# FNet mixing and squared relu on one core: column 128 of seven sequences transformed in one pass instead of one pass each

## The chip, the cores and the metric

The kernel runs on one core of a Trainium2 chip. Times are device microseconds (us) of one execution. Ratios are the mean time of one kernel's fast runs over the mean of the fast runs of the kernel before in the same rounds, so they are not quite the ratios of the medians quoted beside them. PE is TensorE's matmuls, PEld its weight loads, DVE the vector engine, ACT the scalar engine, SP the engine that issues most DMAs here.

## The reference, cut to what matters

```python
X = np.fft.fft(np.fft.fft(x, axis=1), axis=2).real   # x: (8, 3008, 256) float32
h = X.reshape(24064, 256) @ w_in                     # w_in: (256, 2048)
g = np.maximum(h, 0) ** 2
out = g @ w_out                                      # w_out: (2048, 256)
```

The weights arrive as float64.

## The kernel before

The transform over the 256 columns is folded into w_in once. The transform over the 3008 rows is done for each sequence b as matmuls with cosine and sine tables. Symmetry folds x to 753 rows and to columns 0..128: P takes columns 0..127 (cosine), Q takes 1..127 (sine), and column 128 has a transform of its own, E. E enters h as a product of one row, which DVE adds, and so it must lie alike on all 128 partitions. The kernel gets that by copying column 128 of the folded x to 128 stationary columns (wE), so that the matmul itself spreads it:

```python
def fold(b, t):                      # tile t of sequence b; DVE, with two small copies on ACT
    ...
    nc.scalar.copy(wE[r], wP[r, :, H:H + 1].to_broadcast([rows, 2, P]))
    folded[b, t] = (wP, wQ, wE)
...
for kp in range(2):                  # parity of k
    for which in range(3):           # P, Q, E: each an even_n and an odd_n item of three matmuls
        ops += group(kp, which, {})
```

The main loop runs 96 units for each sequence: 6 blocks of columns k by 16 chunks of d_ff. A unit makes h (front), and three units later the output matmuls of an earlier unit follow (back). In between, the folds and the transform of the *next* sequence are strewn in as "side work", evenly over 88 of the 96 units:

```python
for i, (k0, n, fc) in enumerate(units):
    if b == 0 and k0 == 0 and fc % 2 == 0:
        load_wout(fc)                # DVE rounds a piece of w_out from float64
    flight.append((b, k0, n, fc, front(b, k0, n, fc)))
    if len(flight) > LAG:            # LAG = 3
        back(*flight.pop(0))
    upto = min(len(side), len(side) * (i + 1) // (len(units) - 8))
    for f in side[done:upto]:
        f()
    done = upto
```

Of the kernel before, what the change touches and what calls it, by code (L numbers as in the profile page):

```python
# [7 lines left out]
F32 = mybir.dt.float32  # L8
U32 = mybir.dt.uint32
AF = mybir.ActivationFunctionType  # L10
ALU = mybir.AluOpType
PSUM = bass.MemoryType.PSUM
P = 128

# With P(k, m) = sum_n x[n, m] cos(2 pi k n / S) and Q(k, m) the same with sin,
#   Re FFT2(x)[k, d] = sum_m P(k, m) cos(2 pi m d / D) - Q(k, m) sin(2 pi m d / D).
# * The transform over d is linear and sits before w_in, so it is applied to w_in, once:
#   h[k] = P(k) @ (cosD @ w_in) - Q(k) @ (sinD @ w_in).
# * cos and sin are even and odd in m, so columns m and D - m of x fold: P keeps m = 0..128 and
#   Q keeps m = 1..127. Column 128 of P, called E, has a one-row product with w_in, added apart.  # L20
# * P is even and Q is odd in k, so k = 0..S/2 gives all rows: h[S - k] = P-part - Q-part.
# * In n, the rows n, S - n, S/2 - n and S/2 + n share a table row for k of one parity: x folds to
#   n = 0..S/4. With even n in A and odd n in B, P(S/2 - k) = A - B where P(k) = A + B
#   (Q: B - A), so that tables are needed for k = 0..S/4 alone.
# The weights come as float64, of which the chip has no arithmetic: their bits are sent, and rounded
# to float32 on the chip.


def row_tiles(S):
    """Even n, then odd n, of 0..S/4, in tiles of at most 128 rows: (first row, rows) of the folded order."""  # L30
    q = S // 4
    tiles, at = [], 0
    for count in (q // 2 + 1, q // 2):
        assert 2 * P < count <= 3 * P
        for r in range(0, count, P):
            tiles.append((at + r, min(P, count - r)))
        at += count
    return tiles
# [3 lines left out]
def kernel(  # L42
# [12 lines left out]
    nc = tc.nc  # L55
    B, NROW, _, D = x.shape
    S = out.shape[0] // B
    M = S // 2
# [16 lines left out]
    hp = ctx.enter_context(tc.tile_pool(name="hp", bufs=3))  # L75
    gp = ctx.enter_context(tc.tile_pool(name="gp", bufs=5))
    op = ctx.enter_context(tc.tile_pool(name="op", bufs=4))
    psh = ctx.enter_context(tc.tile_pool(name="psh", bufs=3, space=PSUM))
    psd = ctx.enter_context(tc.tile_pool(name="psd", bufs=2, space=PSUM))
    pso = ctx.enter_context(tc.tile_pool(name="pso", bufs=3, space=PSUM))  # L80
# [1 line left out]
    tt = nc.vector.tensor_tensor  # L82
    act = nc.scalar.activation

# [1 line left out]
    xt = {}  # L86

    def load_x(b, t):
# [19 lines left out]
        for tab, src in ((cosT, cos_s), (sinT, sin_s)):  # L108
            nc.gpsimd.dma_start(out=tab[:, kp], in_=src[:, kp])

# [1 line left out]
    def rounded(dst, src):  # L112
        """The float32 next to each float64 of src, [128, 2, 256] of them as 64-bit words in DRAM."""
        if src.dtype == F32:
            nc.sync.dma_start(out=dst, in_=src)
            return
        raw = op.tile([P, 2, CH, 2], U32, name="raw", tag="raw", bufs=2)
        nc.sync.dma_start(out=raw.rearrange("p a b w -> p a (b w)"), in_=src.bitcast(U32))
        low, high = raw[:, :, :, 0], raw[:, :, :, 1]

        def temp(tag):
            t = fp.tile([P, 2, CH], F32, name=tag, tag=tag)
            return t, t.bitcast(U32)

        # Sign, exponent and the first 20 bits of the fraction, to float32's places.
        top, topb = temp("fs")
        nc.vector.tensor_scalar(out=topb, in0=high, scalar1=3, scalar2=0x3FFFFFF8,  # L127
                                op0=ALU.logical_shift_left, op1=ALU.bitwise_and)
        nc.vector.scalar_tensor_tensor(out=topb, in0=high, scalar=0xC0000000, in1=topb,  # L129
                                       op0=ALU.bitwise_and, op1=ALU.bitwise_or)  # L130
        # The other 32 bits as a number, in units of 2^-52 of the signed power of two.
        rest, restb = temp("fd")
        nc.vector.tensor_scalar(out=restb, in0=topb, scalar1=0xFF800000, scalar2=None, op0=ALU.bitwise_and)  # L133
        nc.vector.scalar_tensor_tensor(out=rest, in0=low, scalar=2.0 ** -52, in1=rest, op0=ALU.mult, op1=ALU.mult)  # L134
        tt(out=top, in0=top, in1=rest, op=ALU.add)  # L135
        # Exponents out of float32's range: to zero and to infinity.
        over, _ = temp("fs")
        _, expb = temp("fd")
        nc.vector.tensor_scalar(out=expb, in0=high, scalar1=20, scalar2=0x7FF,  # L139
                                op0=ALU.logical_shift_right, op1=ALU.bitwise_and)  # L140
        nc.vector.tensor_scalar(out=over, in0=expb, scalar1=1150.5, scalar2=2.0 ** 127,  # L141
                                op0=ALU.is_gt, op1=ALU.mult)
        nc.vector.scalar_tensor_tensor(out=top, in0=expb, scalar=896.5, in1=top, op0=ALU.is_gt, op1=ALU.mult)  # L143
        nc.vector.scalar_tensor_tensor(out=dst, in0=over, scalar=1.0, in1=top, op0=ALU.max, op1=ALU.mult)  # L144

# [1 line left out]
    WC = 512  # L147
    for c in range(F // WC):
        cs = slice(c * WC, (c + 1) * WC)
# [17 lines left out]
        rounded(wout[:, fc:fc + 2],  # L167
                moe_w_out[fc * P:(fc + 2) * P].rearrange("(c p) e -> p c e", p=P))

# [1 line left out]
    folded = {}  # L171
    PQE = {}

    def fold(b, t):
        """Rows n, S - n, M - n, M + n and columns m, D - m of x, to the terms of even and of odd k."""
        rows = TILES[t][1]
        r = slice(0, rows)
        v = xt[b, t]
        s = fp.tile([P, 2, D], F32, name="fs", tag="fs")
        d = fp.tile([P, 2, D], F32, name="fd", tag="fd")  # L180
        tt(out=s[r], in0=v[r, 0::2], in1=v[r, 1::2], op=ALU.add)
        tt(out=d[r], in0=v[r, 0::2], in1=v[r, 1::2], op=ALU.subtract)  # L182
        if b + 1 < B:
            load_x(b + 1, t)
        sc = fp.tile([P, 2, H + 1], F32, name="sc", tag="sc")
        dc = fp.tile([P, 2, H - 1], F32, name="dc", tag="dc")
        nc.scalar.copy(sc[r, :, 0:H + 1:H], s[r, :, 0:H + 1:H])
        tt(out=sc[r, :, 1:H], in0=s[r, :, 1:H], in1=s[r, :, D - 1:H:-1], op=ALU.add)
        tt(out=dc[r], in0=d[r, :, 1:H], in1=d[r, :, D - 1:H:-1], op=ALU.subtract)
        wP = wp.tile([P, 2, H + 1], F32, name="wP", tag="wP")  # L190
        wQ = wp.tile([P, 2, H - 1], F32, name="wQ", tag="wQ")
        wE = wp.tile([P, 2, P], F32, name="wE", tag="wE")
        for kp in range(2):
            tt(out=wP[r, kp], in0=sc[r, 0], in1=sc[r, 1], op=ALU.subtract if kp else ALU.add)  # L194
            tt(out=wQ[r, kp], in0=dc[r, 0], in1=dc[r, 1], op=ALU.add if kp else ALU.subtract)
        nc.scalar.copy(wE[r], wP[r, :, H:H + 1].to_broadcast([rows, 2, P]))  # L196
        folded[b, t] = (wP, wQ, wE)

    def dft_ops(b):
        """P, Q and, on all partitions alike, E, for k = 0..M."""  # L200
        ops = []

        def start():
# [2 lines left out]

        def group(kp, which, st):
            nk = NK[kp]
            n = P - 1 if which == 1 else P
            tab = sinT if which == 1 else cosT  # L210

            def product(half):
                ps = psd.tile([P, 512], F32, name="pd", tag="d")[0:n, 0:nk]
                for i in range(3):
                    t = 3 * half + i
                    rows = TILES[t][1]
                    nc.tensor.matmul(ps, folded[b, t][which][0:rows, kp, 0:n], tab[0:rows, kp, t, 0:nk],  # L217
                                     start=i == 0, stop=i == 2)
                return ps

# [4 lines left out]

            def odd_n():
                ps = product(1)
                a, dst = st["a"], PQE[b][which]
                nh = S // 8
                tt(out=dst[:, kp:kp + 2 * nk - 1:2], in0=a, in1=ps, op=ALU.add)  # L230
                hi = dst[:, M - kp - 2 * (nh - 1):M - kp + 1:2][:, ::-1]
# [5 lines left out]
            return [even_n, odd_n]  # L237

        for kp in range(2):
            for which in range(3):  # L240
                ops += group(kp, which, {})
        return [start] + ops

# [1 line left out]
    def front(b, k0, n, fc):  # L245
        pt, qt, et = PQE[b]
        fs = slice(fc * P, (fc + 1) * P)
# [19 lines left out]
    def back(b, k0, n, fc, g):  # L267
# [11 lines left out]
        for s, (g0, cnt, row) in enumerate(sides):  # L279
# [5 lines left out]
            for j, o in enumerate(range(0, cnt, P)):  # L285
                m = min(P, cnt - o)
                nc.scalar.copy(os_[0:m, j], po[s][0:m, j])
                nc.sync.dma_start(out=out[row + o:row + o + m], in_=os_[0:m, j])

    def ahead(b):  # L290
        return [lambda t=t: fold(b, t) for t in range(NT)] + dft_ops(b)

    for f in ahead(0):
        f()
# [3 lines left out]
    for b in range(B):  # L298
        side = ahead(b + 1) if b + 1 < B else []
        done = 0  # L300
        for i, (k0, n, fc) in enumerate(units):
            if b == 0 and k0 == 0 and fc % 2 == 0:
                load_wout(fc)
            flight.append((b, k0, n, fc, front(b, k0, n, fc)))
            if len(flight) > LAG:
                back(*flight.pop(0))
# [11 lines left out]


def _tables(S, D):  # L320
    """The cosines and sines of the transforms, which depend on the shapes alone."""
    import numpy as _np

    q = S // 4
    n = _np.concatenate([_np.arange(0, q + 1, 2), _np.arange(1, q + 1, 2)])
    weight = _np.where((n == 0) | (n == q), 0.5, 1.0)[:, None]  # their four rows of x are two rows twice
    tabs = _np.zeros((2, P, 2, 6, q // 2 + 1), _np.float32)
    for kp in range(2):
        k = _np.arange(kp, q + 1, 2)
# [46 lines left out]
```

## Time and profile before

| | before |
|---|---|
| time, median | 2299.17 us |
| PE busy | 2213.2 us, 96% |
| DVE busy | 1182.4 us, 51% |
| ACT busy | 1049.4 us, 46% |
| E matmuls, 8 sequences | 192 records, about 7.6 us a sequence |

The prediction shows the lines that carry the reading. Kernel before:

```profile
PEld po L275 <- ACT os L282: 6.1, 33, 0.2
PEld po L275 <- ACT os L287: 2.0, 7, 0.3
```

These are the block ends. The second bank of a new block is free only when ACT has copied the old one. Each such wait was 0.2 us at most (0.3 us on the second line, the short last block of a sequence, which is the same after the change), so it looked harmless.

### The profile page before, as it was taken

How to read it: one execution, taken by the hardware profiler on the slowest of the kernel's cores; microseconds unless marked ns; L12 is line 12 of the kernel's file. 1: busy time of each engine (PE TensorE's matmuls, PEld its weight loads, DVE VectorE, ACT ScalarE, POOL GpSimd, SP SyncE). 2: the span in 40 equal slices, each digit the busy share in tenths (PEclk: the TensorE clock that was granted, in tenths of full speed). 3: DMA queues.
4: the chain of work that ended last, by engine and by line, in shares of the span. 5: the costliest groups of instructions: out<-in, count | busy, mean ns of one | idle time of the engine just before them, and what ended most of it. 6: DMA issues, size and time to landing. Idle time of an engine off the chain costs nothing.

```text
span 2298.1 us, 26257 instructions
## 1 busy us (share of the span) xinstructions
PE 2213.2 (96%) x9888; PEld 1865.0 (81%) x9888; DVE 1182.4 (51%) x2932; ACT 1049.4 (46%) x1809; POOL 28.1 (1%) x56
## 2 busy tenths in 40 slices
PE   3679999999999999999999999999999999999998
PEld 1357888888888888888888888888888888888887
DVE  5597444654446544474445644465444644444443
ACT  0124444554445444454445544455444544445554
POOL 0000000000000000000000000000000000000000
PEclk7789999999999999999999999999999999999999
DMA  6221000110001000010000100010000000000000
GB/s 212 72 74 45 19 10 10 36 46 10 10 10 54 28 10 10 28 54 10 19 10 27 55 10 10 10 52 30 10 10 18 10 10 10 19 9 10 19 10 18
DMA packets 38528, 64.29 MB, mean 28 GB/s; under 512 B 3448, under 2 KB 27768, under 8 KB 37888
## 3 DMA queue, kind: packets, MB, share of 16 engines
q1 hardware_dynamic: 30096, 33.04, 4.5%
q0 software_dynamic: 7488, 29.31, 4.2%
q8 instruction: 77, 1.26, 0.2%
q14 instruction: 51, 0.42, 0.1%
q10 hardware_dynamic: 816, 0.26, 0.1%
HBM read 37.96 MB, written 24.64 MB: 27 GB/s over the span
## 4 chain that ended last, share of the span: by engine, by line
PE 94%; DVE 5%; ACT 0%; DMA 0%; issue 0%; ACTq 0%; DVEq 0%
PE po L275 57%; PE ph L252 14%; PE ph L251 14%; PE pd L217 8%; PE pg L157 1%; DVE fs L129 0%; DVE fd L134 0%; DVE fs L135 0%; DVE fs L143 0%; DVE fd L133 0%; DVE fs L141 0%; PE pe L162 0%; DVE fs L127 0%; DVE win L144 0%; DVE fd L139 0%; DVE wout L144 0%
## 5 line engine op out<-in xcount | busy, mean ns | idle before, releaser
L275 PE MATMUL po<-wout,g 128*128 128x256 f32 (+1 forms) x6144 | 1460.2, 380 | 1.1 <-ACT g L262 1.1
L275 PEld LDWEIGHTS po<-wout,g 128*128 128x128 f32 (+1 forms) x6144 | 1150.2, 188 | 177.9 <-ACT os L282 6.1
L261 ACT ACTIVATE g<-g 128x512 f32<-128x512 f32 (+2 forms) x768 | 476.2, 620 | 1010.8 <-DVE g L259 983.0
L254 DVE SCALAR_TENSOR_TENSOR he<-Et,gE,ph 128x256 f32<-128x256 f32 (+1 forms) x768 | 364.2, 474 | 859.8 <-PE ph L252 859.2
L262 ACT ACTIVATE g<-g 128x512 f32<-128x512 f32 (+2 forms) x768 | 477.1, 621 | 24.4
L251 PE MATMUL ph<-Pt,G 128*128 128x256 f32 (+1 forms) x1536 | 453.6, 377 | 19.5 <-DVE g L259 19.5
L252 PE MATMUL ph<-Qt,G 127*128 127x256 f32 (+1 forms) x1536 | 453.5, 376 | 0.0
L251 PEld LDWEIGHTS ph<-Pt,G 128*128 128x128 f32 x1536 | 292.8, 191 | 82.3 <-DVE g L259 22.8
L258 DVE TENSOR_TENSOR g<-he,ph 128x256 f32<-128x256 f32 (+1 forms) x768 | 319.5, 416 | 67.3 <-DVE he L254 4.1
L252 PEld LDWEIGHTS ph<-Qt,G 127*128 127x128 f32 x1536 | 294.5, 192 | 33.5
L259 DVE TENSOR_TENSOR g<-he,ph 128x256 f32<-128x256 f32 (+2 forms) x768 | 314.2, 409 | 0.0
L217 PE MATMUL pd<-cosT,wP 128*128 128x377 f32 (+3 forms) x192 | 70.7, 502 | 8.4 <-DVE wP L194 6.0
L217 PE MATMUL pd<-sinT,wQ 128*127 128x377 f32 (+3 forms) x192 | 67.5, 490 | 0.0
L217 PE MATMUL pd<-cosT,wE 128*128 128x377 f32 (+3 forms) x192 | 65.7, 479 | 0.0
L217 PEld LDWEIGHTS pd<-cosT,wP 128*128 128x128 f32 (+1 forms) x192 | 37.0, 197 | 30.7 <-DVE wP L194 8.8
L157 PE MATMUL pg<-win,cosd 128*128 128x512 f32 x16 | 14.9, 1083 | 47.4 <-DVE win L144 47.4
L217 PEld LDWEIGHTS pd<-sinT,wQ 128*127 128x127 f32 (+1 forms) x192 | 37.3, 194 | 20.1 <-issue 1.5
L217 PEld LDWEIGHTS pd<-cosT,wE 128*128 128x128 f32 (+1 forms) x192 | 36.5, 190 | 19.1
L196 ACT COPY wE<-wP 128x256 f32<-128x256 f32 (+2 forms) x48 | 19.4, 403 | 70.0 <-DVE wP L194 70.0
L224 ACT COPY da<-pd 128x377 f32<-128x377 f32 (+3 forms) x48 | 22.7, 473 | 57.3 <-PE pd L217 57.3
L157 PEld LDWEIGHTS pg<-win,cosd 128*128 128x128 f32 x16 | 4.7, 324 | 51.8 <-DVE win L144 26.2
L91 POOL DMA_DIRECT2D xt<-in_x_dram x48 | 25.6, 536 | 1537.8 <-DVE fd L182 1537.0
(38 smaller groups left out, 396.0 us busy)
## 6 DMA issues: line engine op xcount, KB each, us to landing
out_dram<-os SPq DMA_DIRECT2D x72, 256.0 KB
xt<-in_x_dram POOLq DMA_DIRECT2D x32, 512.0 KB, 3.8
raw<-in_moe_w_in_dram SPq DMA_DIRECT2D x8, 512.0 KB
raw<-in_moe_w_out_dram SPq DMA_DIRECT2D x8, 512.0 KB
xt<-in_x_dram POOLq DMA_DIRECT2D x8, 484.0 KB, 4.5
xt<-in_x_dram POOLq DMA_DIRECT2D x8, 480.0 KB, 4.5
out_dram<-os SPq DMA_DIRECT2D x24, 128.0 KB
cosT<-in_cos_s_dram POOLq DMA_DIRECT2D x2, 1131.0 KB, 18.4
```

The lines of the kernel that those rows point to most:

```text
L91: nc.gpsimd.dma_start(out=xt[b, t][0:rows], in_=x[b, r0:r0 + rows])
L157: nc.tensor.matmul(ps[0:n], tab[:, i], w[:, i], start=i == 0, stop=i == 1)
L217: nc.tensor.matmul(ps, folded[b, t][which][0:rows, kp, 0:n], tab[0:rows, kp, t, 0:nk], start=i == 0, stop=i == 2)
L224: nc.scalar.copy(st["a"], ps)
L251: nc.tensor.matmul(hP, G1[:, fs], pt[:, ks], start=True, stop=True)
L252: nc.tensor.matmul(hQ, G2[:, fs], qt[:, ks], start=True, stop=True)
L254: nc.vector.scalar_tensor_tensor(out=t, in0=et[:, ks], scalar=gE[:, fc:fc + 1], in1=hP, op0=ALU.mult, op1=ALU.add)
L258: tt(out=g[:, 0:n], in0=t, in1=hQ, op=ALU.add)
L259: tt(out=g[:, n:n + hi - lo][:, ::-1], in0=t[:, lo:hi], in1=hQ[:, lo:hi], op=ALU.subtract)
L261: act(g, g, AF.Relu)
L262: act(g, g, AF.Square)
L275: nc.tensor.matmul(po[s][0:m, j], g[:, g0 + o:g0 + o + m], wout[:, fc], start=fc == 0 and j == 0, stop=fc == NFC - 1, skip_group_check=True)
```

## The change

E of sequences 1 to 7 is a transform of seven columns of numbers. The change reads those columns straight from x (4 bytes at a time), folds them together, transforms them in *one* pass whose stationary operand is 7 columns wide, stores the seven rows in DRAM, and later loads each row spread over 128 partitions. Sequence 0 keeps its own pass. The core of the diff (removed comments left out):

```diff
+    def load_column(t):
+        ...
+        for i in range(4):
+            nc.sync.dma_start(out=xe[t][0:rows, i], in_=x[1:B, r0:r0 + rows, i, H].rearrange("b r -> r b"))
+    def fold_column(t): ...          # three small DVE operations: xe -> es -> we, 7 columns wide
-        nc.scalar.copy(wE[r], wP[r, :, H:H + 1].to_broadcast([rows, 2, P]))
+        if b == 0:
+            nc.scalar.copy(wE[r], wP[r, :, H:H + 1].to_broadcast([rows, 2, P]))
 ...
-            for which in range(3):
+            for which in ((2,) if b is None else (0, 1) if b else (0, 1, 2)):
                 ops += group(kp, which, {})
+        if b is None:
+            return ops + [lambda: nc.sync.dma_start(out=e_dram[:, :], in_=e_rows)]
 ...
+    def load_e(b):
+        nc.sync.dma_start(out=PQE[b][2], in_=e_dram[b - 1:b].to_broadcast([P, NKT]))
     def ahead(b):
-        return [lambda t=t: fold(b, t) for t in range(NT)] + dft_ops(b)
+        ops = [lambda t=t: fold(b, t) for t in range(NT)] + dft_ops(b)
+        if b == 1:
+            ops += [lambda t=t: fold_column(t) for t in range(NT)] + dft_ops(None)
+        return ops + [lambda: load_e(b)] if b else ops
 ...
+            if b == 0 and NFC <= i < NFC + NT:
+                load_column(i - NFC)
```

The rule that spreads the side work is not edited, but the lengths of its lists are: 27 items instead of 19 for sequence 1, 16 instead of 19 for the others.

More of the change, by code (lines that the diff above doesn't have):

```diff
@@ L77 @@
     op = ctx.enter_context(tc.tile_pool(name="op", bufs=4))
+    dp = ctx.enter_context(tc.tile_pool(name="dp", bufs=1, space=bass.MemoryType.DRAM))
     psh = ctx.enter_context(tc.tile_pool(name="psh", bufs=3, space=PSUM))
@@ L172, with fold_column @@
     PQE = {}
+    NE = B - 1
+    xe, we = {}, {}
+    e_dram = dp.tile([NE, NKT], F32, name="e_dram")
+    e_rows = const.tile([NE, NKT], F32, name="e_rows")
+    def load_column(t):
+        r0, rows = TILES[t]
+        xe[t] = const.tile([P, 4, NE], F32, name=f"xe{t}")
+        for i in range(4):
+            nc.sync.dma_start(out=xe[t][0:rows, i], in_=x[1:B, r0:r0 + rows, i, H].rearrange("b r -> r b"))
+    def fold_column(t):
+        rows = TILES[t][1]
+        r = slice(0, rows)
+        v = xe[t]
+        s = fp.tile([P, 2, NE], F32, name="es", tag="es")
+        tt(out=s[r], in0=v[r, 0::2], in1=v[r, 1::2], op=ALU.add)
+        we[t] = const.tile([P, 2, NE], F32, name=f"we{t}")
+        for kp in range(2):
+            tt(out=we[t][r, kp], in0=s[r, 0], in1=s[r, 1], op=ALU.subtract if kp else ALU.add)
     def fold(b, t):
@@ L191, in fold @@
         wQ = wp.tile([P, 2, H - 1], F32, name="wQ", tag="wQ")
-        wE = wp.tile([P, 2, P], F32, name="wE", tag="wE")
+        wE = wp.tile([P, 2, P], F32, name="wE", tag="wE") if b == 0 else None
         for kp in range(2):
@@ L208, in group @@
             nk = NK[kp]
-            n = P - 1 if which == 1 else P
+            n = NE if b is None else P - 1 if which == 1 else P
             tab = sinT if which == 1 else cosT
@@ L216, in product @@
                     rows = TILES[t][1]
-                    nc.tensor.matmul(ps, folded[b, t][which][0:rows, kp, 0:n], tab[0:rows, kp, t, 0:nk],
+                    w = we[t] if b is None else folded[b, t][which]
+                    nc.tensor.matmul(ps, w[0:rows, kp, 0:n], tab[0:rows, kp, t, 0:nk],
                                      start=i == 0, stop=i == 2)
@@ L227, in odd_n @@
                 ps = product(1)
-                a, dst = st["a"], PQE[b][which]
+                a, dst = st["a"], e_rows if b is None else PQE[b][which]
                 nh = S // 8
```

## The prediction

> **What bounds the kernel now.** I read the engine shares first, then the busy time by stretch, then the PE timeline inside one stretch. The shares say which engine is nearly always busy:
>
> ```profile
> PE 2213.2 (96%) x9888; PEld 1865.0 (81%) x9888; DVE 1182.4 (51%) x2932; ACT 1049.4 (46%) x1809; POOL 28.1 (1%) x56
> PE 94%; DVE 5%; ACT 0%; DMA 0%; issue 0%; ACTq 0%; DVEq 0%
> ```
>
> The second line is the chain that ended last: TensorE (PE) for 94%, the vector engine (DVE) for 5%. An average hides where each of the two rules, so I cut the span into windows (busy us and instruction counts by engine, then the granted clock, DMA share and GB/s):
>
> ```profile
> 117.00:188.00 71.00, 50.36 (x182) 38.84 (x181) 67.82 (x150) 21.85 (x40) 1.59 (x3) 0.87 0.20 67
> 188.00:2290.00 2102.00, 2101.68 (x9533) 1792.77 (x9531) 1051.93 (x2646) 1014.92 (x1743) 17.56 (x33) 1.00 0.07 20
> 2290.00:2298.10 8.10, 0.00 (x0) 0.00 (x0) 0.00 (x0) 0.36 (x2) 0.00 (x0) 0.68 0.25 57
> ```
>
> From 188 us to 2290 us TensorE is busy 2101.68 of 2102 us at the full clock. There the time is simply the sum of the matmuls: a matmul taken out is worth its whole duration, and vector, scalar or DMA work taken out is worth nothing. From 117 to 188 us it is the other way round: DVE is busy 67.82 of 71 us and TensorE idles 20.6 us. This is the first output block of sequence 0, in which DVE also converts the eight pieces of w_out. There added DVE work costs its whole duration. Before 117 us (w_in, first transform) and after 2290 us (last copy and store) the change touches nothing.
>
> What one group of E costs in the long stretch is read from the timeline of PE (start, length, what, count). The listed lengths overlap at their ends, so the start of the next row is what counts:
>
> ```profile
> 579.96 1.89 PE L275 MATMUL po<-wout,g 128*128 128x256 f32 x8
> 581.68 2.07 PE L217 MATMUL pd<-cosT,wE 128*128 128x377 f32 x6
> 583.59 0.59 PE L251 MATMUL ph<-Pt,G 128*128 128x256 f32 x2
> 584.02 0.59 PE L252 MATMUL ph<-Qt,G 127*128 127x256 f32 x2
> 584.46 1.89 PE L275 MATMUL po<-wout,g 128*128 128x256 f32 x8
> 586.18 0.60 PE L251 MATMUL ph<-Pt,G 128*128 128x256 f32 x2
> ```
>
> The group of three matmuls (six records; a float32 matmul leaves two) takes 583.59 - 581.68 = 1.91 us. The unit behind it takes 586.18 - 583.59 = 2.59 us, as the units without a transform beside them do, so the group costs its own time and no more. A group on 376 columns is 1.90 us in the same view (593.96 to 595.86, a P group).
>
> **What the Trainium skill says.** "TensorE: Matmul & The Clock Gate", section "Back-to-back issue gap", gives N/2.4 + 2.5 ns warm, N being the streamed columns. The width of the stationary operand is not in it. Counting four passes per float32 matmul, an assumption, 377 columns give 4 x 377/2.4 = 628 ns; the trace has 1.91/3 = 637 ns, near it. So a stationary operand of 7 columns should cost TensorE as much as one of 128: the gain is that one pass serves seven sequences, not that the pass is narrow. The same page, "LDWEIGHTS", makes weight loading proportional to the columns, which would shorten only the loads, already hidden here.
> "DMA: Bandwidth & Descriptors", "Rules for kernel authors", says that a strided last dimension "Lowers to one descriptor per element". The reads of column 128 are of this kind, and nothing in the trace of before shows its cost at volume. The skill's "Specifications" of that page adds that below 512 B a transfer is a read-modify-write. The trace gives an upper neighbour: queue q1 moved 30096 packets, about 1.1 KB each, in 4.5% of 16 x 2298 us = 1655 us, so 55 ns per packet. I take 55 ns for a 4-byte one too, as an estimate.
>
> **The change, part by part.**
> 1. Removed on TensorE: the E groups of sequences 1 to 7. Each sequence had four: two parities of k, two halves of n; two on 377 and two on 376 columns: 2 x 1.91 + 2 x 1.90 = 7.62 us. All lie in the stretch bound by TensorE. 7 x 7.62 = 53.3 us.
> 2. Added on TensorE: one such pass, stationary operand 7 wide, moving operand unchanged: 7.62 us. Net 45.7 us less.
> 3. Removed on ACT and DVE: for each of seven sequences, six wE copies (403 ns), two copies from PSUM and four writes of Et. All of it ran beside a full TensorE: worth 0.
> 4. Moved: the side work of a sequence is spread evenly over 88 of the 96 units. For sequence 1 the list grows from 19 to 27 items (27 = 6 folds, start, 8 groups, 6 column folds, 4 E groups, store, load), so its folds come closer together. The built order of DVE shows it: in before, three folds (after units 4, 9, 13) lie ahead of the last w_out conversion; in after there are four (after units 3, 6, 9, 13). One more fold is pulled into the stretch that DVE bounds. The DVE timeline shows a fold there from 137.88 to 140.89, 156.97 to 160.05 and 174.97 to 178.04 us: mean 3.05 us. It is paid in full, since what DVE is spared later is spare time. Cost 3.05 us.
> 5. Added DMA: 24 column reads, each of 7 x (120 to 128) elements of 4 bytes, about 21,100 descriptors. Divided over engines: about 56 each when 16 share, some 77 where 121 rows allow only 11, so near 1,430 on the busiest engine; at 55 ns that is 79 us. They start on the SP queue when the last w_out load has been issued, near 173 us. The first column fold stands behind unit 52, which I place at 188 + 36 x 2.595 + 8 x 1.9 = 297 us; the last, behind unit 68, near 342 us. So 120 to 170 us are there for 79. Hidden.
> 6. Added: six column folds of three tiny DVE operations, the store of 42 KB and seven loads of E spread over 128 partitions (0.77 MB). Each load is placed 9 units, 23 us, ahead of its first use; the x loads of 0.5 MB land in 3.8 us, so some 6 to 8 us is likely. Hidden.
>
> Sum: 2299.17 - 53.3 + 7.6 + 3.05 = 2256.5 us, that is 1.86% less.
>
> **The rivals.**
> (a) The column reads are slow. DVE then stops at a column fold, soon TensorE after it, once the four units in flight are used up. It takes more than about (342 - 173)/1430 = 118 ns per 4-byte descriptor; each further 10 ns then adds 14 us. For it: the read-modify-write and the 1 to 4 KB stride in DRAM. Against it: twice the 55 ns estimate is needed. At 150 ns the stall would be 45 us and the whole gain gone: about 2300 us.
> (b) The extra fold costs nothing or less, because TensorE, not DVE, ends the early stretch. For it: after 184.45 us TensorE ran some matmuls at half pace (1.22 us for a pair that takes 0.60 later) and DVE waited 3.18 us for it. Against it: that wait comes after the last conversion; before it DVE has no gap over 0.31 us, so the fold delays everything behind it. If free, 2253.4 us, right on the 2% line.
> (c) The E loads arrive late, or the outputs are held up behind the column reads on the shared SP queue. At the end of a block, outputs have four buffers, two used per block of 16 units (41 us), so a delay under 80 us is not felt. I would expect at most a few us.
> (d) The 7-wide pass is quicker than the wide one. It could give back at most 7.6 us: 2249 us.
>
> **Range and chances.** The matmul sum is firm to about 0.5 us; the early stretch to about 3 us, since the half-pace moments of the clock may fall differently; the runs of before spread by 2 us. Hence 2252 to 2263 us, the upper side a little longer for (a) and (c). Faster by over 2% means below 2253.2 us, which needs (b) or (d): 0.10. Slower needs (a) at over 200 ns per descriptor: 0.02. Within 2%: 0.88.
>
> **What would show it.** Right: E groups with a 7-wide output take 1.9 us start to start; PE busy falls by about 46 us; from the end of the early stretch to the end PE still shows no idle time; DVE's conversions end about 3 us later (the last w_out conversion ended at 183.2 us in before). Wrong: a wait of DVE on the column tile es<-xe, or of he on Et for a DMA; PE idle time between 250 and 350 us or at the start of a sequence; a 7-wide group well under 1.9 us; conversions ending no later than before.

## More of the kernel before

At the last chunk of a block ACT copies the two finished output banks out of PSUM. There are three such banks, and a block uses two. The lines of waits say who waited for whom on TensorE's weight loads, us in total, times, longest.

## The result, and the profile after

| | before | after |
|---|---|---|
| time, median | 2299.69 us (4 runs) | 2262.0 us (4 runs, 2261.26 to 2262.97) |
| ratio | | 0.9837 (95%: 0.9824 to 0.9851) |
| span of the profiled run | 2298.1 us | 2260.8 us |
| PE busy | 2213.2 us | 2172.9 us |

The kernel is 1.6% faster, 37.7 us, within 2% and inside the stated range. But it missed the predicted 2256.5 us by 5.5 us, several times the scatter of the runs. PE busy fell by 40.3 us instead of the 46 that the prediction named as a sign.

To find the 5.5 us I lined up the two traces unit by unit, by the start of each unit's first matmul, and took the differences. This is the whole account:

| stretch | before | after | difference | predicted |
|---|---|---|---|---|
| up to unit 0 of sequence 0 | 115.49 | 116.14 | +0.65 | 0 |
| unit 0 to unit 20 of sequence 0 (the w_out stretch and the first block end) | 79.77 | 82.65 | +2.88 | +3.05 |
| unit 20 to unit 94 of sequence 0 (4 wide E groups before, 4 narrow ones after) | 213.44 | 214.65 | +1.21 | 0 |
| each of the six sequences after, unit 94 to unit 94 | 270.47 | 263.49 | -6.98 | -7.62 |
| the last sequence, without side work, from its predecessor's unit 94 to its own | 247.86 | 247.85 | 0 | 0 |

Six times -6.98 instead of -7.62 loses 3.9 us, and the narrow groups lose 1.2 us. The first row is scatter: over all fourteen traces, those of the experiments too, unit 0 started between 114.5 and 116.8 us, whatever the kernel.

First the parts that went as foreseen. The windows that answer to those of before (busy us and counts of PE, PEld, DVE, ACT, POOL, then clock, DMA share, GB/s), kernel after:

```profile
117.00:191.50 74.50, 52.73 (x186) 40.82 (x185) 71.12 (x158) 20.55 (x38) 2.13 (x4) 0.84 0.32 71
191.50:2252.60 2061.10, 2059.51 (x9389) 1758.96 (x9387) 1040.95 (x2634) 992.76 (x1689) 17.03 (x32) 1.00 0.08 23
```

The stretch bound by DVE is longer by about a fold, and from there on TensorE is busy again all the time but for 1.6 us. The DMA part was hidden completely. Kernel after, the column tile (durations in ns as min/median/max, then first and last start in us) and the landing times in the list of DMA issues:

```profile
L186 SPq DMA_DIRECT2D xe<-in_x_dram x24: 465/562/3653, 167.6 to 213.2; - x24
L193 DVE TENSOR_TENSOR es<-xe x6: 168/168/168, 299.4 to 341.0; 128x14 f32<-128x14 f32 x4, 121x14 f32<-121x14 f32 x1, 120x14 f32<-120x14 f32 x1
...
Et<-e_dram SPq DMA_DIRECT2D x7, 752.5 KB, 4.4
xe<-in_x_dram SPq DMA_DIRECT2D x16, 3.5 KB, 2.7
```

The last column read was issued at 213.2 us, a read landed in 2.7 us (median), and the first use was at 299.4 us.

Now the two terms that were off. **The narrow group**, in the timeline of kernel after; start, length, what, count, and in brackets the idle time before it:

```profile
347.32 1.89 PE L303 MATMUL po<-wout,g 128*128 128x256 f32 x8
349.14 0.10 PEld L243 LDWEIGHTS pd<-cosT,we 128*7 128x7 f32 x2 [0.33 <-issue]
349.14 2.07 PE L243 MATMUL pd<-cosT,we 128*7 128x377 f32 x6
349.46 0.09 PEld L243 LDWEIGHTS pd<-cosT,we 128*7 128x7 f32 x1 [0.23 <-issue]
...
351.13 0.30 PEld L279 LDWEIGHTS ph<-Pt,G 128*128 128x128 f32 x2 [0.64 <-issue]
351.14 0.70 PE L279 MATMUL ph<-Pt,G 128*128 128x256 f32 x2
351.67 0.60 PE L280 MATMUL ph<-Qt,G 127*128 127x256 f32 x2
```

From 349.14 to 351.14 is 2.00 us where a wide group took 1.91. There is also a step at either edge. The output matmuls before began at 347.32 and such a set takes 1.73 us, so the group could have begun at 349.05, and the pair behind it takes 0.53 us to the next start instead of 0.43. Together that is about 0.3 us more than a wide group. The lengths of the single matmuls are the same, so a table of mean durations does not show it. Starts do.

**The block end**, at unit 18 of sequence 2. Kernel before (its fold stands behind unit 18 itself):

```profile
733.42 0.63 ACT L261 ACTIVATE g<-g 128x512 f32<-128x512 f32 x1 [1.31 <-DVE g L259]
734.08 0.63 ACT L262 ACTIVATE g<-g 128x512 f32<-128x512 f32 x1
734.45 1.92 PE L275 MATMUL po<-wout,g 128*128 128x256 f32 x8
734.62 0.57 ACT L282 COPY os<-po 128x512 f32<-128x512 f32 x1
735.24 0.73 PEld L275 LDWEIGHTS po<-wout,g 128*128 128x128 f32 x4 [0.16 <-ACT os L282]
```

Kernel after (the fold stands behind unit 16):

```profile
725.88 0.68 DVE L205 TENSOR_TENSOR fs<-xt 121x512 f32<-121x512 f32 x1
...
730.30 0.63 ACT L289 ACTIVATE g<-g 128x512 f32<-128x512 f32 x1 [2.87 <-DVE g L287]
730.97 0.63 ACT L290 ACTIVATE g<-g 128x512 f32<-128x512 f32 x1
731.50 0.61 ACT L289 ACTIVATE g<-g 128x512 f32<-128x512 f32 x1
732.15 0.63 ACT L290 ACTIVATE g<-g 128x512 f32<-128x512 f32 x1
732.20 2.23 PE L303 MATMUL po<-wout,g 128*128 128x256 f32 x8
732.68 0.57 ACT L310 COPY os<-po 128x512 f32<-128x512 f32 x1
733.30 0.73 PEld L303 LDWEIGHTS po<-wout,g 128*128 128x128 f32 x4 [0.48 <-ACT os L310]
```

Read it from the top. The fold keeps DVE for 3 us, so the next h is late. ACT idles 2.87 us and then has two units' relu and square back to back, and the copy of the finished bank stands behind them in its queue. Measured from the start of the output matmuls that need the bank, the copy starts 0.48 us after instead of 0.17 us. The weight load waits 0.48 instead of 0.16 us, and the eight output matmuls take 2.23 instead of 1.92 us. The line of waits sums it up, kernel after:

```profile
PEld po L303 <- ACT os L310: 11.1, 33, 1.5
```

This is as many waits as before, 33, but 11.1 us instead of 6.1. One of them, of 1.5 us, is the first block end of sequence 0. The rest is spread over the sequences: while the side work of sequences 2 to 7 runs, the units 19 and 35 of each sequence, each with a fold two units ahead of its block end in the changed kernel, take 2.94 and 2.87 us instead of 2.62 and 2.69, and unit 51 takes 2.74 instead of 2.59. Ahead of unit 51 there is no fold: the kernel before had a Q group right at that block end (behind unit 50), and the changed kernel has none there. Neither DVE nor ACT is a bound by its busy share (52 and 45%). What counts is *when* a 3 us piece of DVE work falls.

**Theory.** The change removed what was foreseen (7.62 us a sequence). Part came back because the shorter lists shifted the side work, which put two folds ahead of block ends and took a group away from one (0.64 us a sequence), and because a group with 7 stationary columns costs TensorE about 0.3 us more than one with 128. **Rivals.** The new DMA traffic disturbs every sequence; the removed groups were never worth 7.62 us; the column reads or column folds cost time of their own.

### The profile page after: what moved, and what is told of

Read it like the earlier page. It is cut to its first block, busy times and chain, and to the rows that moved or that the text cites. A ratio compares the mean times of both kernels' runs of the same rounds, so it can differ in the third digit from the quotient of the medians.

```text
span 2260.8 us, 25972 instructions
## 1 busy us (share of the span) xinstructions
PE 2172.9 (96%) x9744; PEld 1832.7 (81%) x9744; DVE 1174.1 (52%) x2926; ACT 1026.3 (45%) x1755; POOL 28.1 (1%) x56
## 3 DMA queue, kind: packets, MB, share of 16 engines
q1 hardware_dynamic: 52562, 38.56, 5.9%
## 4 chain that ended last, share of the span: by engine, by line
PE 92%; DVE 5%; ACT 1%; DMA 1%; issue 0%; ACTq 0%; DVEq 0%
PE po L303 57%; PE ph L280 14%; PE ph L279 14%; PE pd L243 6%; DMA raw<-in_moe_w_in_dram 1%; PE pg L160 1%; ACT g L289 0%; DVE fs L132 0%; DVE fd L137 0%; DVE fs L138 0%; DVE fs L146 0%; ACT g L290 0%; DVE fd L136 0%; DVE fs L144 0%; DVE fs L130 0%
## 5 line engine op out<-in xcount | busy, mean ns | idle before, releaser
L303 PEld LDWEIGHTS po<-wout,g 128*128 128x128 f32 (+1 forms) x6144 | 1149.1, 188 | 184.4 <-ACT os L310 11.1
L310 ACT COPY os<-po 128x512 f32<-128x512 f32 x72 | 38.3, 577 | 0.0
L250 ACT COPY da<-pd 128x377 f32<-128x377 f32 (+5 forms) x36 | 17.0, 473 | 44.2 <-PE pd L243 44.2
L161 ACT COPY G<-pg 128x512 f32<-128x512 f32 (+1 forms) x8 | 4.7, 586 | 68.9 <-PE pg L160 68.9
L206 DVE TENSOR_TENSOR fd<-xt 128x512 f32<-128x512 f32 (+2 forms) x48 | 32.9, 686 | 0.0
```

Of the source, the lines that this page charges most:

```text
L206: tt(out=d[r], in0=v[r, 0::2], in1=v[r, 1::2], op=ALU.subtract)
L303: nc.tensor.matmul(po[s][0:m, j], g[:, g0 + o:g0 + o + m], wout[:, fc], start=fc == 0 and j == 0, stop=fc == NFC - 1, skip_group_check=True)
L310: nc.scalar.copy(os_, po[s])
```

## The experiments

Each was timed over 3 rounds except the last four below. Beside them the kernel before had medians from 2299.39 to 2299.86 us. Except where said, the results were correct.

**Spacing of sequences 2 to 7 put back.**

```diff
+        if b > 1:
+            ops = ops[:11] + [lambda: None] * 2 + ops[11:] + [lambda: None]
         return ops + [lambda: load_e(b)] if b else ops
```

> The changed kernel with three empty slots put back into the side work of sequences 2 to 7, so that every fold and every P and Q group stands behind the same unit as in the kernel before. Theory (the closer spacing moved folds to two units ahead of a block end, which delays the copy of the finished output bank and makes TensorE wait 0.31 + 0.18 + 0.15 us more at three block ends of each sequence): 6 x 0.64 = 3.9 us less than the changed kernel's 2262.0, so about 2258.1 us, and the step from one sequence to the next in the trace is 7.6 us shorter than before instead of 6.97. Rival 1 (the loads of E through DRAM disturb each sequence): nothing changes, 2262 us. Rival 2 (the removed groups were never worth 7.62 us each sequence): nothing changes either.

Measured: 2258.39 us, ratio 0.9821. A sequence now takes 262.86 us in the trace (one of the six 263.20: DVE has a pause of 0.46 us right at a block end there, of a kind that turns up here and there in every trace), that is 7.61 us less than before's 270.47, so the removed E groups are worth what the sum said to a hundredth. Two rivals fall: the loads of E are all still there, and nothing was wrong with the worth of a group. One window from unit 94 to unit 94 of the same sequence shows it for before, after and this run, in this order (window and its length, then PE, PEld, DVE, ACT, POOL):

```profile
684.16:954.62 270.46, 270.46 (x1226) 230.15 (x1225) 137.80 (x348) 130.25 (x225) 3.20 (x6) 1.00 0.08 24
```

```profile
681.91:945.40 263.49, 263.41 (x1202) 225.29 (x1200) 136.06 (x344) 126.86 (x218) 3.19 (x6) 1.00 0.09 27
```

```profile
681.46:944.32 262.86, 262.86 (x1202) 225.31 (x1200) 135.83 (x344) 126.97 (x218) 3.20 (x6) 1.00 0.09 27
```

PE calls itself busy in all three: the wait hides inside stretched matmul lengths. The length of the window is the evidence, not the busy column.

**The kernel before in the changed kernel's slots.** The other direction: all E groups kept, only the slots of sequences 2 to 7 changed.

```diff
-            upto = min(len(side), len(side) * (i + 1) // (len(units) - 8))
+            n_ops = len(side)
+            when = [-(-(k + 1) * 88 // n_ops) - 1 for k in range(n_ops)]
+            if b > 0:
+                when = [5, 10, 16, 21, 27, 32, 38, 43, 49, 54, 60, 62, 62, 65, 71, 76, 82, 86, 86]
+            upto = len([w for w in when if w <= i])
```

> The kernel before, all of its E groups kept, with the side work of sequences 2 to 7 in the slots of the changed kernel (folds behind units 5, 10, 16, 21, 27, 32). Theory (spacing alone costs 0.64 us a sequence): 3.9 us slower than the kernel before, about 2303.6 us. Rival (the lost time belongs to DMA or to the removed groups): 2299.7 us, as before.

Measured: 2303.0 us, ratio 1.0016 (1.0001 to 1.003). A sequence takes 271.05 us instead of 270.47, 0.58 us more, six times 3.5 us. Spacing alone makes the loss, in a kernel with no new DMA at all.

**Folds away from block ends, and folds two units ahead of them.** Two runs that differ in three folds of each sequence by 4 units.

```diff
+            if b > 0:                       # folds away from block ends
+                when = [5, 12, 21, 28, 37, 44] + [53, 53, 55, 57, 59, 61, 69, 71, 73, 87]
```
```diff
+            if b > 0:                       # three folds two units ahead of a block end
+                when = [5, 16, 21, 32, 37, 48] + [53, 53, 55, 57, 59, 61, 69, 71, 73, 87]
```

> The changed kernel with the folds of sequences 2 to 7 behind units 5, 12, 21, 28, 37 and 44, the P and Q groups behind units 53 to 73 and the load of E at 87: no fold within the three units ahead of a block end (block ends are taken up at units 18, 34, 50, 66, 82). Theory: about 2258 us, block-end waits of TensorE on the copy of the output bank as in the kernel before (0.16 to 0.23 us each). Rival (the spacing is not the cause): 2262 us.

> As the run with no fold near a block end, but three of the six folds of sequences 2 to 7 moved by 4 units to stand two units ahead of a block end (units 5, 16, 21, 32, 37, 48). Theory: each such fold adds 0.2 to 0.3 us, 18 of them 3.5 to 5.5 us, so about 2262.5 us, 4 to 5 us above the run with none. Rival: the same time as that run.

Measured: 2260.01 and 2263.37 us. A sequence takes 263.07 and 263.81 us, so 18 folds cost 6 x 0.74 = 4.4 us, 0.25 us each, as expected. The medians differ by 3.4 us, a little under the expected 4 to 5. The waits, first the run with folds away from block ends, then the run with folds ahead of them:

```profile
PEld po L303 <- ACT os L310: 8.2, 39, 0.2
```

```profile
PEld po L303 <- ACT os L310: 12.6, 39, 0.5
```

The number of waits is equal, and the longest goes from 0.2 to 0.5 us. The position of a fold relative to the block end is the cause. (Each fold also starts the load of the next x tile, which moved with it. No run parts the two, but what the weight loads wait for in the trace is ACT's copy.) The first of the two missed its own mark of 2258 us: 263.07 is above the 262.86 of the first experiment although no fold is near a block end. There were 39 waits here against 33. In the first experiment one Q group of each of the six sequences stood right at a block end (behind unit 50), and unit 51 took 2.59 us; here no group stands at one, and it took 2.68. A group at a block end gives the copy time, on which the last experiment bears.

**The first folds of sequence 1 put back**, so that three and not four lie among the w_out conversions.

```diff
+            n_ops = len(side)
+            when = [-(-(k + 1) * 88 // n_ops) - 1 for k in range(n_ops)]
+            if b == 0:
+                when = [4, 9, 13, 18, 23, 27] + [max(w, 28) for w in when[6:]]
```

> The changed kernel with only the six folds of sequence 1 put back behind units 4, 9, 13, 18, 23 and 27 as in the kernel before, so that three and not four lie ahead of the last conversion of w_out. Theory (the stretch of the conversions is bound by the vector engine, a fold there costs its 3.05 us): about 2259 us, and the last conversion ends 3.0 us earlier than in the changed kernel; a further 1 us may go because the wait of 1.09 us at the first block end has its fold two units ahead too. Rival (TensorE ends that stretch, the fold is free): 2262 us.

Measured: 2258.47 us, ratio 0.9821. The last conversion of w_out, kernel before, after, and this run:

```profile
182.53 0.69 DVE L144 SCALAR_TENSOR_TENSOR wout<-fs 128x512 f32<-128x512 f32 x1
```

```profile
186.25 0.69 DVE L147 SCALAR_TENSOR_TENSOR wout<-fs 128x512 f32<-128x512 f32 x1
```

```profile
183.18 0.69 DVE L147 SCALAR_TENSOR_TENSOR wout<-fs 128x512 f32<-128x512 f32 x1
```

It ends 3.07 us earlier than in the changed kernel (counted from unit 0, which started within 0.03 us in the two traces, 3.10 us), and unit 20 comes 4.35 us earlier after unit 0 (78.30 instead of 82.65 us): the fold, and the wait of about 1.1 us at the first block end, which went with it. The fold was not free.

**The pass on 128 columns.** Seven with data, the rest zeros.

```diff
+        we[t] = wp.tile([P, 2, P], F32, name="wE", tag="wE")
+        nc.gpsimd.memset(we[t], 0.0)
-            n = NE if b is None else P - 1 if which == 1 else P
+            n = P if b is None else P - 1 if which == 1 else P
```

> The changed kernel with the one pass for E on 128 stationary columns, 7 with data and 121 of zeros, instead of 7. Theory (a 7-wide group costs TensorE about 0.3 us more than a wide one, since its short weight loads show idle time before them and the next group's loads come late): each group 1.9 us again, 4 x 0.3 = 1.2 us less in the trace, about 2260.8 us. Rival of the prediction (the width makes no difference, or narrow is quicker): 2262 us or more.

Measured: 2260.75 us, ratio 0.9832. The two ranges just overlap (2260.37 to 2261.61 us, against 2261.26 to 2262.97), so the trace decides: unit 20 to unit 94 of sequence 0 takes 213.60 us instead of 214.65. The group in the timeline of this run:

```profile
347.04 1.89 PE L304 MATMUL po<-wout,g 128*128 128x256 f32 x8
348.77 2.07 PE L244 MATMUL pd<-cosT,wE 128*128 128x377 f32 x6
350.68 0.59 PE L280 MATMUL ph<-Pt,G 128*128 128x256 f32 x2
351.11 0.59 PE L281 MATMUL ph<-Qt,G 127*128 127x256 f32 x2
```

It takes 1.91 us with no step at either edge. Multiplying zeros is faster than not multiplying them.

**Without the pass**: a wrong result (relative error 0.06). The `load_column` calls, column folds and the four E groups were replaced by empty slots and one memset; the store and the seven loads stayed.

> Wrong result on purpose for sequences 1 to 7: no column reads, no column folds, no pass; zeros go to DRAM in its place and the seven loads remain, and all other work keeps its slots. Theory (the pass costs only its four groups on TensorE, 4 x 2.2 = 8.8 us; reads and column folds are hidden): about 2253.2 us. Rival (4-byte reads or column folds cost on their own): less than 2253 us by whatever they cost, say 2248 us if 5 us of the miss were theirs.

Measured: 2252.66 us, ratio 0.9798. Unit 20 to unit 94 takes 205.86 us, 8.79 less than in the changed kernel, against the 4 x 2.2 = 8.8 us of the groups alone. Column reads and column folds cost nothing that shows.

**Twice the reads, twice the loads.** A second column read into tiles that nobody uses, and each load of E issued twice.

> The changed kernel with twice the 4-byte column reads (48 instead of 24, a second column into tiles nobody reads) and every load of E done twice. Theory (both are hidden; the reads land in 2.6 us each and the loads in 4.4 us with 23 us to spare): 2262 us within 1 us. Rival (their contention makes the lost time): about 5 us more, 2267 us.

Measured: 2262.23 us, ratio 0.9838, the same as the changed kernel; a sequence takes 263.48 us. The rival that blames DMA falls.

**Where the narrow pass begins to cost.** The pass on 32, 64 and 65 columns, one look each (state unknown, so the traces count here and not the times).

> The pass for E on 32 stationary columns (7 with data). If the cost of the narrow pass comes from its matmuls using only a part of the array's columns, so that TensorE changes shape before and after each group, it stays: 2.2 us from one unit to the next. If it comes from the very short weight loads (84 to 91 ns at 7 columns against 190 ns at 128), it falls with the width.

> The same on 64 columns. A changed part of the array: still near 2.2 us a group. Short loads: about half way, 2.05 us.

> The same on 65 columns. A changed part of the array: 1.91 us a group, as at 128 columns, since half the columns are exceeded. Short loads: as at 64 columns.

| columns | unit with a group | unit behind it | unit 20 to unit 94 | one time |
|---|---|---|---|---|
| 7 | 4.69 us | 2.70 us | 214.65 us | (2262.0, 4 runs) |
| 32 | 4.71 | 2.70 | 214.72 | 2261.74 |
| 64 | 4.73 | 2.70 | 214.81 | 2262.92 |
| 65 | 4.50 | 2.59 | 213.60 | 2261.70 |
| 128 | 4.50 | 2.59 | 213.60 | (2260.75, 4 runs) |

It is a step between 64 and 65 columns, not a slope. Short weight loads are not the reason: at 65 columns they are short and have idle time before them as well, at no cost. The 65-column run:

```profile
349.29 2.07 PE L244 MATMUL pd<-cosT,wE 128*65 128x377 f32 x6
349.61 0.14 PEld L244 LDWEIGHTS pd<-cosT,wE 128*65 128x65 f32 x1 [0.18 <-issue]
351.20 0.60 PE L280 MATMUL ph<-Pt,G 128*128 128x256 f32 x2
```

That up to half of the stationary columns makes TensorE work in another shape, and that going into and out of it costs the 0.3 us, fits all five rows, but it is argued and not shown. There are always as many PSUM partitions written as stationary columns, and no run parts these two.

**All of it together.** The pass on 128 columns, no fold before unit 20 of sequence 0, no fold ahead of a block end, odd P and Q groups right at block ends; timed over 5 rounds.

```diff
+            if b == 0:
+                when = ([20, 23, 26, 29, 36, 39] + [40, 42, 50, 52, 54, 57, 59, 61, 66] +
+                        [68, 69, 70, 71, 72, 73] + [75, 77, 79, 82] + [83, 86])
+            else:
+                when = [4, 7, 10, 20, 23, 26] + [28, 29, 34, 42, 50, 58, 66, 74, 82] + [84]
+            upto = len([w for w in when if w <= i])
```

> What the runs so far point to, put together in the changed kernel: the pass for E on 128 columns; no fold of sequence 1 before unit 20, so none among the conversions of w_out; folds of sequences 2 to 7 behind units 4, 7, 10, 20, 23, 26, none ahead of a block end; and the odd P and Q groups exactly at the block ends 34, 50, 66 and 82, where their 1.9 us of matmuls give the copy of the output bank time. Theory, against the changed kernel's 2262.0: four folds out of the early stretch 4 x 3.05 = 12.2 us, pass 1.2 us, spacing 6 x 0.64 = 3.8 us, block ends covered by groups some 2 to 3 us: about 2242 to 2245 us, faster than the kernel before by over 2%. Rival for the early stretch (beyond the first fold TensorE ends it): 2250 us.

Measured: 2243.3 us (2242.0 to 2243.61, 5 runs), ratio 0.9753 (0.974 to 0.9767), 2.5% faster than before and faster than every other run with a correct result. Units 0 to 20 take 69.0 us, 13.65 less than in the changed kernel, so TensorE did not end the early stretch when all four folds had gone. The last conversion ends 59.20 us after unit 0 instead of 70.80, 11.6 us earlier for four folds (12.2 expected), and until then DVE is still busy 56.18 us and PE only 45.94; the other 2 us lie between it and unit 20, where the wait at the first block end is gone and the granted clock is 1.00 instead of 0.86. A sequence takes 262.78 us (one of the six 263.14, with the same kind of DVE pause), only 0.08 less than with the old spacing. The waits on the copy shrank to this:

```profile
PEld po L304 <- ACT os L311: 3.2, 13, 0.6
```

There are 13 waits instead of 33: groups at a block end do cover the copy. But the 2 to 3 us expected from it came out near 6 x 0.08 = 0.5 us. The reason can be read from the starts: a unit behind a block end with a weight load's wait of about 0.2 us takes 2.62 to 2.69 us instead of 2.59, so TensorE loses only 0.03 to 0.1 us of it, and there was little to win. The early stretch made up for it.

## Why the prediction was right or wrong

- *TensorE bounds the kernel from the w_out stretch to the end; a removed group is worth its duration.* Right: 7.61 us a sequence with the old spacing, against 7.62. But that PE is listed as busy 2101.68 of 2102 us does not say that it waits for nothing: 33 waits, 6.1 us of weight loads, lie in that stretch of the kernel before.
- *The one new pass costs 7.62 us.* Too small: 8.79 us. The failed step here is the reading that a stationary operand of 7 columns should cost TensorE as much as one of 128. Rival (d) even had it quicker. Up to 64 columns it is about 0.3 us a group slower.
- *One more fold among the conversions costs 3.05 us, paid in full.* Right. Counted from unit 0, the last conversion ended after 67.73 us in the kernel before, 70.80 us after the change and 67.70 us with the fold taken back. Rival (b), a free fold, fell. That the whole stretch up to unit 20 came out at +2.88 us, near 3.05, is partly luck: two things that the prediction did not have nearly cancel. The changed kernel waits 1.09 us at the first block end, which has a fold two units ahead. And in the trace of the kernel before the granted clock behind the last conversion was low for longer: 0.72 over the 12.04 us up to unit 20, where two other traces with the same early work (the kernel before in the changed kernel's slots, and the first folds put back) have 0.84 and take 10.62 and 10.60 us. With 0.86 in the changed kernel, the put-back compares nearly equal clocks, and there the fold and the wait together were worth 4.35 us.
- *The moved side work.* This is the main step that failed, by 3.9 us, the largest part of the miss. The prediction followed the spacing for sequence 1 alone, where DVE is the bound. For the other six it rested on "vector, scalar or DMA work taken out is worth nothing", and took work that is only *moved* there as free too. Moving a 3 us fold to two units ahead of a block end costs 0.25 us, through DVE, ACT's queue and the copy of the output bank. In the changed kernel two such folds (0.32 and 0.18 us) and one group that no longer stands at a block end (0.15 us) make the 0.64 us of a sequence.
- *Column reads and E loads hidden.* Right, with more room than thought: all reads were issued by 213.2 us for a first use at 299.4, and doubling both changed nothing. The use time had been estimated at 297 us. The estimate of 55 ns for each 4-byte read was far too high (the last section works out 7 to 10 ns). Rivals (a) and (c) did not come about. The upper side of the range had been kept for these two; that the time still lies inside, 1 us from its end, for other reasons, is luck.

Together: 3.9 + 1.2 us, and 0.65 us of scatter at the start, less 0.2 us in the early stretch, make the 5.5 us.

Of the pages cited: "TensorE: Matmul & The Clock Gate", "Back-to-back issue gap", agrees for groups wider than 64 columns (637 ns against the 628 ns worked out, or 638 with the four times 2.5 ns that the prediction left out; the four passes stay an assumption). Its formula has no term for the width, and the measurement decides against leaving it out. "LDWEIGHTS", loading in proportion to the columns, is not borne out: 84 to 91 ns with 7 columns, 187 to 193 ns with 128. "DMA: Bandwidth & Descriptors", "Rules for kernel authors", one descriptor per element, agrees: queue q1 had 52562 packets with the pass and 31118 without it, 21444 more, against 7 x 753 x 4 = 21084 elements. Whether a 4-byte read is a read-modify-write, as the prediction takes from "Specifications", no run here shows.

## What to carry to other kernels

When an edit changes how many items an even-spacing rule spreads, every item moves. List where each long item lands relative to the places where a buffer must come free, before counting the removed work as gained. On an engine that calls itself busy all the time, measure from start to start of the repeating unit, since a short wait hides inside the listed lengths. And try a narrow stationary operand padded to over half the columns before believing that narrow is cheap.

## What the Trainium skill lacked or had wrong

- "TensorE: Matmul & The Clock Gate", sections "Back-to-back issue gap" and "LDWEIGHTS": they lack that a group of float32 matmuls with up to 64 stationary columns, between groups with 128, costs more: 2.2 us against 1.91 us for three matmuls of 377 columns, with a step between 64 and 65 columns. "TensorEngine Tiling (Array Packing)", section "Key Properties", has that changing the tiling mode drains TensorE, but no time for it, and not that one narrow group among wide ones would be such a change; whether it is the cause here is not shown.
- "TensorE: Matmul & The Clock Gate", "LDWEIGHTS": the time of a load was not in proportion to the columns here, 84 to 91 ns with 7 and 187 to 193 ns with 128.
- "DMA: Bandwidth & Descriptors", "Rules for kernel authors": the count of descriptors is right, but the page has no time for reads of 4 bytes (the nearest is about 10.5 ns per packet for a transfer of 4 KB, in its section "Bandwidth"). Here reads of 896 elements landed in 2.7 us (median) each. The 21444 extra packets raised q1's share of 16 engines from 5.4 to 5.9%, about 8 ns of engine time each (5.9% less 5.4% of 16 x 2261 us is 181 us; the rounded shares leave it between 7 and 10 ns).
